# Attention backward on one core: O and wo transposed by DMA instead of TensorE, and half of K on TensorE

## The chip, the cores and the metric

One Trainium2 chip, one of its cores. The metric is the device time of one launch in microseconds, the median of several runs. The kernel is written by hand, with tiles, pools of buffers and an explicit order of emission; the time of before is the median of three runs on the chip.

## The reference

Two independent attention blocks A and B are computed forward and backward, and their outputs stand side by side. One block, for B = 8 batches, H = 32 heads, Sq = 96 queries, Sk = 512 cached keys, Dh = 128 and D = 640, all in bfloat16:

```
q   = (x @ wq) split into heads          # [8, 32, 96, 128]
s   = q @ k_cache^T * Dh**-0.5           # [8, 32, 96, 512]
p   = softmax(s)
o   = p @ v_cache                        # [8, 32, 96, 128]
out = concat of heads of o @ wo          # [8, 96, 640]
```

`reference()` returns the output (blocks side by side, [8, 96, 1280]) and, for a given `grad_out`, the gradients of x, k_cache, v_cache, wq and wo of both blocks. The gradients of the caches have the caches' size, 8 x 32 x 512 x 128 each, so the kernel reads some 161 MB from HBM and writes some 159 MB.

## The kernel before, in words

**Units of work.** A chunk is one head h and one batch b: 96 queries against 512 keys. The chunks run in the order of heads, and within a head of batches, first all of block A (32 heads), then all of block B. Time is divided into ticks; chunk n starts at tick n. The stages of one chunk are spread over several ticks, so that in each tick each engine works on several chunks at different stages (the table `OFF`): keys loaded 5 ticks ahead (`ldk`), values 3 ahead (`ldv`), S and softmax at tick 3 after the chunk's own (`c_s2a`, `c_s2b`, `c_s3a`, `c_s3b`), P transposed and dV at 4 (`c_s45`, `c_s4`), O at 5, dP and dS at 6 (`c_s6`), dK and dS transposed at 7 (`c_s7`, `c_s8`), dQ at 8 (`c_s8`). K and V come in pairs of batches, one DMA for two chunks.

**Order.** Every piece is added to `Emitter` with a tick and a slot within the tick, and the pieces are emitted in the order of (tick, slot). Each engine works its own instructions off in order, with two exceptions: S and softmax are raised in priority (`tc.high_priority`), and instructions in `pinned(...)` keep the program's place on their queue. DMAs of SP's queue are pinned: the loads of K and V (slot 0), the transposing DMAs (slot 1), the stores of dV and dK (slot 1.5), all of a tick before the next tick's.

**Transposes of K and V.** dP needs V transposed and S needs K transposed. V is always transposed by a DMA from SBUF to SBUF (`c_xt`, tile `VT`, one DMA for two chunks, at the tick of the first). For K, `k_on_pe(h, b)` decides: for the first pair of batches of each head, and for some whole heads at the start of a block, TensorE transposes it chunk by chunk (`c_s1`, four transposes of 128 x 128 into PSUM, copied by VectorE to `KT_pe`); the other pairs go by DMA (`KT`, issued three ticks ahead of the chunk's own).

**Work once per head.** Pieces with the slot `SL_HEAD` come after the chunk stages of a tick; their ticks (table `HK`) count from the head's first chunk. At -10 and -9 the head's parts of wq and wo are loaded from POOL's queue (`pA`, `pA2`; tile `wo_h`). At -3, `pB` transposes wo (five transposes into `woT_ps`, copied by ScalarE to `woT_h`) and wq (the same, by VectorE, to `wqT_h`). From -2 to 0, `pC` projects Q from wq and dO from `woT_h` (matmuls `q_ps`; dO's first 512 columns at tick -1). At 1 and 2, `pD` brings dO and Q to natural layout. After the head's chunks, `qA(h, 1)` at 17 and `qA(h, 0)` at 18 transpose dQ and O of the head to natural layout (six transposes each into `nat_ps`; O is copied by ScalarE to `Onat`, dQ by VectorE to `dQnat`). At 19 and 20, `qB` computes dwo from `Onat` (matmuls `dwo_ps`); at 18, 19 and 21, in odd heads, `qD` computes dwq for two heads. So in a steady state each tick belongs to a head's phase: tick t and tick t + 8 do the same work for consecutive heads, and tick -3 of the next head is tick 5, tick 18 of the last one is tick 2.

**Work once per group of heads.** Heads are taken in groups of at most five. After a group, `gU` multiplies the group's O with wo and dQ with wq (matmuls `o_ps`), adding into accumulators of out and dx; these pieces are spread over some 18 ticks, so that some heads have much of this work and others none.

**Buffers.** All matmul results go through eight banks of PSUM, used in rotation. `woT_h` and `Onat` have one buffer each; `KT` has three, `VT` four.

Of the kernel before, what the change touches and what calls it, by code (L numbers as in the profile page):

```python
# [11 lines left out]
BF16 = mybir.dt.bfloat16  # L12
# [28 lines left out]
SL_HEAD = 90  # L41
# [1 line left out]
SL_SETUP = 96  # L43

OFF = dict(ldk=-5, ldv=-3, kt=-3, vt=0, s2=3, s3=3, s4=4, s5=5, s6=6, s7=7, s8=8)
HK = dict(pA=-10, pA2=-9, pB=-3, pC0=[-2, 0], pC1=[-1, 0], pD1=1, pD0=2, qA0=18, qA1=17, qB=[19, 20], qD=[(18, 0, 2), (19, 2, 4), (21, 4, 5)])
EV = dict(pB0="act", pB1="dve", pC00="act", pC01="act", pC10="act", pC11="dve", pD0="dve", pD1="dve", qA0="act", qA1="dve", qB0="act", qB1="dve", qD="dve", gU="act")
GSPREAD0 = 9
PRIO_OFF = 2000
# [4 lines left out]
def build_block(tc, em, tick0, blk, x, kc, vc, wq, wo, g_all, out_all, dx, dk, dv, dwq, dwo, ident, ones, pools, HG=6, first=True, groups=None):  # L54
# [43 lines left out]
    def bank(shape, dt, name):  # L98
        return ps.tile(shape, dt, name=name, tag="bank")
# [11 lines left out]
    def pinned(ins):  # L111
        return tc.keep_in_program_order(ins)
# [42 lines left out]
    def evac(eng, dst, src, sc=None):  # L155
        if eng == "act":
            nc.scalar.activation(dst, src, ACT.Identity, scale=(1.0 if sc is None else sc))
        else:
            if sc is None:
                nc.vector.tensor_copy(dst, src)  # L160
            else:
                nc.vector.tensor_scalar(dst, src, float(sc), None, op0=ALU.mult)
# [33 lines left out]
    def pA2(h):  # L196
        def f():
            wo_h = hst.tile([128, D], BF16, name="wo_h", bufs=HG + 3)
            ld = nc.gpsimd.dma_start(wo_h[:], wo[h * 128:(h + 1) * 128, :])
            if not (first and h == 0):  # L200
                pinned(ld)
            HS[(blk, h)]["wo_h"] = wo_h
        return f

    def pB(h):
        def f():
            st = HS[(blk, h)]
            woT_ps = bank([128, DC * 128], BF16, "woT_ps")
            for c in range(DC):
                nc.tensor.transpose(woT_ps[:, c * 128:(c + 1) * 128], st["wo_h"][:, c * 128:(c + 1) * 128], ident[:])  # L210
            woT_h = hd.tile([128, DC * 128], BF16, name="woT_h", bufs=1)
            evac(EV["pB0"], woT_h[:], woT_ps[:])
            st["woT_h"] = woT_h
            wqT_ps = bank([128, DC * 128], BF16, "wqT_ps")
            for c in range(DC):
                nc.tensor.transpose(wqT_ps[:, c * 128:(c + 1) * 128], st["wq_h"][:, c, :], ident[:])
            wqT_h = hst.tile([128, D], BF16, name="wqT_h")
            evac(EV["pB1"], wqT_h[:], wqT_ps[:])
            st["wqT_h"] = wqT_h
            st["slot"] = (blk * H + h) % OD.shape[2]  # L220
            st["OT_h"] = OD[:, 0, st["slot"]]
            st["dQT_h"] = OD[:, 1, st["slot"]]
            st["QT_h"] = hd.tile([128, T], BF16, name="QT_h")
            st["dOT_h"] = hd.tile([128, T], BF16, name="dOT_h")
        return f
# [199 lines left out]
    def c_s7(h, b):  # L425
# [9 lines left out]
            nc.scalar.activation(SB[(blk, h, b // 2, "k")][:, b % 2], dK_ps[:], ACT.Identity, scale=1.0)  # L435
        return f

    def qA(h, which):
        def f():
            st = HS[(blk, h)]  # L440
            src = st["OT_h"] if which == 0 else st["dQT_h"]
            if which == 0:
                dst = hd.tile([128, TT, 128], BF16, name="Onat", bufs=1)
                st["Onat"] = dst
            else:
                if h % 2 == 0:
                    st["dQnat"] = hd.tile([128, TT, 2, 128], BF16, name="dQnat", bufs=1)
                else:
                    st["dQnat"] = HS[(blk, h - 1)]["dQnat"]
                dst = st["dQnat"][:, :, h % 2, :]  # L450
            for t0 in range(0, TT, 8):
                nt = min(8, TT - t0)
                n_ps = bank([128, 8 * 128], BF16, "nat_ps")
                for i in range(nt):
                    nc.tensor.transpose(n_ps[:, i * 128:(i + 1) * 128], src[:, (t0 + i) * 128:(t0 + i + 1) * 128], ident[:])  # L455
                evac(EV["qA%d" % which], dst[:, t0:t0 + nt, :], n_ps[:, 0:nt * 128].rearrange("p (t d) -> p t d", d=128))
        return f
# [88 lines left out]
    NTS = len(tsplits)  # L546

    def k_on_pe(h, b):
        return b // NB == 0 or h == 0 or (first and h == 1)

    SX = pools["SX"]
    for g in range(NG):
        h0 = GH0[g]
        for hh in range(groups[g]):
            h = h0 + hh
            c0t = tick0 + h * B
            if not (first and h == 0):
                em.add(c0t + HK["pA"], 54.6, pA(h))
                em.add(c0t + HK["pA2"], 54.6, pA2(h))
            em.add(c0t + HK["pB"], SL_HEAD, pB(h))  # L560
            fh = first and h == 0
            p0, p1, d1, d0, late = HK["pC0"], HK["pC1"], HK["pD1"], HK["pD0"], 0
            if fh:
                p1, d1, d0, late = [3, 3], 3, 4, 7
            elif h == 0:
                p0, p1, d1, d0, late = [-2, 2], [0, 3], 3, 4, 7
            for si in range(NTS):
                em.add(c0t + p0[min(si, 1)], SL_HEAD, pC(h, 0, si))
                em.add(c0t + p1[min(si, 1)], SL_HEAD + late, pC(h, 1, si))
            em.add(c0t + d1, SL_HEAD + (8 if late else 0), pD(h, 1))  # L570
            em.add(c0t + d0, SL_HEAD, pD(h, 0))
            for b in range(B):
                ct = c0t + b
                if b % NB == 0:
                    em.add(tick0 - 12 if first and h == 0 and b == 0 else ct + OFF["ldk"], SLOTS["LOAD"], c_ld(h, b, "K", 7))
                    em.add(ct + OFF["ldv"], SLOTS["LOAD"], c_ld(h, b, "V", 5))
                    if not k_on_pe(h, b):
                        em.add(ct + OFF["kt"], SLOTS["LOAD"] + 1, c_xt(h, b, "KT", 3))
                    em.add(ct + OFF["vt"], SLOTS["LOAD"] + 1, c_xt(h, b, "VT", 4))
                if k_on_pe(h, b):  # L580
                    em.add(ct + 2, SLOTS["S1"], c_s1(h, b))
                em.add(ct + OFF["s2"], SLOTS["S2A"], c_s2a(h, b))
                em.add(ct + OFF["s2"], SLOTS["S2B"], c_s2b(h, b))
                em.add(ct + OFF["s3"], SLOTS["S3A"], c_s3a(h, b))
                em.add(ct + OFF["s3"], SLOTS["S3B"], c_s3b(h, b))
                em.add(ct + OFF["s5"], SLOTS["S5B"], c_s5b(h, b))
                if b % 2 == 1:
                    em.add(ct + OFF["s4"] + 1, SLOTS["LOAD"] + 1.5, c_st(h, b, "v"))
                    em.add(ct + OFF["s7"] + 1, SLOTS["LOAD"] + 1.5, c_st(h, b, "k"))
                em.add(ct + OFF["s4"], SLOTS["S4"], c_s4(h, b))  # L590
                for i, o in enumerate(("s8", "s7", "s5", "s4")):
                    SX.setdefault(ct + OFF[o], [None] * 4)[i] = (blk, h, b)
                em.add(ct + OFF["s6"], SLOTS["S6"], c_s6(h, b))
                em.add(ct + OFF["s7"], SLOTS["S7"], c_s7(h, b))
            hk = HK if first or h < H - 1 else dict(HK, qA0=13, qB=[14, 15], qA1=16, qD=[(19, 0, 2), (19, 2, 4), (19, 4, 5)])
            em.add(c0t + hk["qA0"], SL_HEAD, qA(h, 0))
            for di in range(len(wsplits)):
                em.add(c0t + hk["qB"][di], SL_HEAD + 1, qB(h, di))
            em.add(c0t + hk["qA1"], SL_HEAD, qA(h, 1))
            for (k_, c_lo, c_hi) in hk["qD"]:  # L600
                if c_lo < DC and h % 2 == 1:
                    em.add(c0t + k_, SL_HEAD + 2, qD(h, c_lo, min(c_hi, DC)))
        cLg = tick0 + (h0 + groups[g] - 1) * B + B - 1
        gs0 = max(3, (GSPREAD0 * groups[g]) // HG)
        gs1 = max(3, (GSPREAD1 * groups[g]) // HG)
        if not first and g == NG - 2:
            gs0, gs1 = 9, 9
        if g == 0:
            em.add(cLg + OFF["s5"] - 2, SL_LOAD, setup_acc)
        subs = [(0, t, gi) for t in range(TT) for gi in range(len(gsplits))] + [(1, t, gi) for t in range(TT) for gi in range(len(gsplits))]  # L610
        n_out = TT * len(gsplits)
        for i, (which, t, gi) in enumerate(subs):
            if which == 0:
                tk = cLg + OFF["s5"] + 2 + (i * gs0) // n_out
            else:
                tk = cLg + OFF["s8"] + 2 + gs0 - 3 + ((i - n_out) * gs1) // n_out
            em.add(tk, SL_GRP, gU(g, which, t, gi))
# [124 lines left out]
```

## Time and profile before

| What | Value |
|---|---|
| Time, median of 3 runs | 1671.19 us (1670.91 to 1674.83) |
| Profiled execution, its own time | 1669.93 us |
| Its span, first to last instruction | 1668.1 us |
| Mean granted TensorE clock | 0.999 |
| TensorE matmuls (PE) | busy 1638.2 us, 98% of the span |
| TensorE weight loads (PEld) | busy 1318.2 us, 79% |
| VectorE (DVE) | busy 1303.1 us, 78% |
| ScalarE (ACT) | busy 1392.7 us, 83% |
| GpSimd (POOL) | busy 663.8 us, 40% |
| HBM | 161.09 MB read, 159.12 MB written |
| Transposing DMAs | 256 VT, 183 KT |
| Median from issue to landing | VT 5.1 us, KT 5.0 us, loads of K 4.3 to 4.4 us |

How to read it: busy time is the union of an engine's instructions, and a row of a group gives the busy time, the mean duration of one instruction in ns, and the idle time of the engine just before them with what ended it. Matmuls overlap, so the mean duration of one (219 ns for 128 columns) is longer than the distance to the next. DMA issues stand on the engine that issues them (SPq is SP's queue), with the time that the issuing took. A window's row has the length, the busy time and number of instructions of PE, PEld, DVE, ACT and POOL, the granted clock, the DMA engines' share and the rate in GB/s.

### The profile page before, as it was taken

How to read it: one execution, taken by the hardware profiler on the slowest of the kernel's cores; microseconds unless marked ns; L12 is line 12 of the kernel's file. 1: busy time of each engine (PE TensorE's matmuls, PEld its weight loads, DVE VectorE, ACT ScalarE, POOL GpSimd, SP SyncE). 2: the span in 40 equal slices, each digit the busy share in tenths (PEclk: the TensorE clock that was granted, in tenths of full speed). 3: DMA queues.
4: the chain of work that ended last, by engine and by line, in shares of the span. 5: the costliest groups of instructions: out<-in, count | busy, mean ns of one | idle time of the engine just before them, and what ended most of it. 6: DMA issues, size and time to landing. Idle time of an engine off the chain costs nothing.

```text
span 1668.1 us, 56047 instructions
## 1 busy us (share of the span) xinstructions
PE 1638.2 (98%) x21355; PEld 1318.2 (79%) x21536; DVE 1303.1 (78%) x2978; ACT 1392.7 (83%) x3518; POOL 663.8 (40%) x1235
## 2 busy tenths in 40 slices
PE   8999999999999999999999999999999999999998
PEld 7887787787788787887878778877877877877886
DVE  6886777778788788888888767878878778787787
ACT  7998897797798796978879898978977977977975
POOL 3444343343343343434344333433433433433432
PEclk9999999999999999999999999999999999999999
DMA  9999999999999999999999999999999999998994
GB/s 275 259 294 277 233 275 278 243 284 271 239 269 272 247 284 249 269 259 264 292 261 283 286 282 247 292 260 244 279 276 225 276 270 244 282 284 230 246 285 147
DMA packets 763151, 439.03 MB, mean 263 GB/s; under 512 B 483776, under 2 KB 753472, under 8 KB 762880
## 3 DMA queue, kind: packets, MB, share of 16 engines
q1 hardware_dynamic: 750256, 392.32, 98.9%
q0 software_dynamic: 12624, 43.10, 8.4%
q8 instruction: 169, 2.77, 0.7%
q14 instruction: 102, 0.84, 0.2%
HBM read 161.09 MB, written 159.12 MB: 192 GB/s over the span
## 4 chain that ended last, share of the span: by engine, by line
PE 81%; ACT 10%; issue 4%; DVE 3%; DMA 1%; POOL 0%; SPq 0%; ACTq 0%; DVEq 0%; POOLq 0%
PE q_ps L243 12%; PE o_ps L512 11%; PE dwq_ps L490 6%; PE dK_ps L432 6%; PE dV_ps L389 6%; PE dP_ps L417 5%; PE S_ps L298 5%; PE dst_ps L346 5%; PE dwo_ps L470 4%; PE x_ps L365 4%; PE x_ps L359 4%; PE x_ps L340 4%; PE n_ps L258 3%; PE nat_ps L455 2%; ACT E_sb L310 2%
## 5 line engine op out<-in xcount | busy, mean ns | idle before, releaser
L329 POOL TENSOR_SCALAR P_sb<-E_sb,rinv 96x512 bf16<-96x512 bf16 x512 | 352.2, 688 | 873.6 <-DVE rinv L320 842.6
L310 ACT ACTIVATE E_sb<-S_ps,negm 96x512 bf16<-96x512 f32 x512 | 353.5, 690 | 164.3 <-DVE negm L300 162.3
L421 DVE SCALAR_TENSOR_TENSOR dS_sb<-dP_ps,dl_ps,P_sb 96x512 bf16<-96x512 f32 x512 | 381.1, 744 | 47.3 <-PE dl_ps L419 42.9
L300 DVE TENSOR_REDUCE negm<-S_ps 96x1 f32<-96x512 f32 x512 | 347.7, 679 | 48.0 <-PE S_ps L298 45.7
L435 ACT ACTIVATE dK_sb<-dK_ps 128x512 bf16<-128x512 f32 x512 | 304.9, 595 | 73.6 <-PE dK_ps L432 72.6
L392 ACT ACTIVATE dV_sb<-dV_ps 128x512 bf16<-128x512 f32 x512 | 314.0, 613 | 0.0
L378 ACT ACTIVATE PT_sb<-x_ps 128x384 bf16<-128x384 bf16 x512 | 255.7, 499 | 0.0
L512 PEld LDWEIGHTS <-OD 128*128 128x128 bf16 x1536 | 135.7, 98 | 103.2 <-issue 1.3
L389 PE MATMUL dV_ps<-dOnat_h,P_sb 96*128 96x128 bf16 x2048 | 198.2, 219 | 1.3 <-DVE dOnat_h L160 0.6
L432 PE MATMUL dK_ps<-Qnat_h,dS_sb 96*128 96x128 bf16 x2048 | 198.1, 219 | 0.0
L417 PE MATMUL dP_ps<-VT,dOT_h 128*96 128x512 bf16 x512 | 195.2, 381 | 0.0
L407 POOL TENSOR_TENSOR prod<-OD,dOT_h 128x96 bf16<-128x96 bf16 x512 | 184.8, 361 | 8.9 <-ACT OD L375 8.6
L348 DVE COPY dST_sb<-dst_ps 128x384 bf16<-128x384 bf16 x512 | 177.3, 346 | 12.6 <-PE dst_ps L346 12.3
L320 DVE RECIPROCAL rinv<-rowsum 96x1 f32<-96x1 f32 x512 | 79.9, 156 | 130.3 <-ACT E_sb L310 125.5
L346 PE MATMUL dst_ps<-ident,dS_sb 96*128 96x96 bf16 x2048 | 172.0, 206 | 2.1 <-DVE dS_sb L421 0.2
L365 PE MATMUL x_ps<-ident,P_sb 96*128 96x96 bf16 x2048 | 171.9, 205 | 1.6 <-POOL P_sb L329 1.3
L375 ACT ACTIVATE OD<-x_ps 128x192 bf16<-128x192 f32 (+1 forms) x515 | 170.5, 331 | 3.4 <-PE x_ps L340 3.4
L359 PE MATMUL x_ps<-PT_sb,V_sb 128*128 128x96 bf16 x2048 | 172.4, 206 | 0.5 <-ACT PT_sb L378 0.5
L340 PE MATMUL x_ps<-dST_sb,K_sb 128*128 128x96 bf16 x2048 | 170.9, 206 | 0.0
L340 PEld LDWEIGHTS <-K_sb 128*128 128x128 bf16 x2048 | 132.7, 98 | 32.1
L298 PE MATMUL S_ps<-KT,QT_h 128*96 128x512 bf16 x366 | 138.7, 379 | 2.6 <-DMA KT<-K_sb 2.3
L512 PE MATMUL o_ps<-wo_h,OD 128*128 128x128 bf16 (+1 forms) x705 | 134.0, 292 | 3.3
(82 smaller groups left out, 3352.4 us busy)
## 6 DMA issues: line engine op xcount, KB each, us to landing
out_dram<-dV_sb SPq DMA_DIRECT2D x256, 256.0 KB, 4.1
out_dram<-dK_sb SPq DMA_DIRECT2D x256, 256.0 KB, 4.5
K_sb<-in_A_k_cache_dram SPq DMA_DIRECT2D x128, 256.0 KB, 4.4
V_sb<-in_A_v_cache_dram SPq DMA_DIRECT2D x128, 256.0 KB, 4.2
K_sb<-in_B_k_cache_dram SPq DMA_DIRECT2D x128, 256.0 KB, 4.3
V_sb<-in_B_v_cache_dram SPq DMA_DIRECT2D x128, 256.0 KB, 4.1
out_dram<-dwo_sb POOLq DMA_DIRECT2D x63, 160.0 KB, 3.9
out_dram<-dwq_sb POOLq DMA_DIRECT2D x31, 320.0 KB, 5.4
```

The source lines that it names most:

```text
L300: nc.vector.tensor_reduce(negm[:], S_ps[:], axis=AX.X, op=ALU.max, negate=True)
L310: nc.scalar.activation(E_sb[:], st["S_ps"][:], ACT.Exp, bias=st["negm"][:], scale=1.0, accum_out=rowsum[:])
L329: pinned(nc.gpsimd.tensor_scalar(P_sb[:], st["E_sb"][:], st["rinv"][:], 0.0, op0=ALU.mult, op1=ALU.add))
L340: nc.tensor.matmul(dQT_ps, st["K_sb"][:, c, :], st["dST_sb"][:, c * Sq:(c + 1) * Sq], start=(c == 0), stop=(c == KC - 1))
L378: nc.scalar.activation(PT_sb[:], PT_ps, ACT.Identity, scale=1.0)
L389: nc.tensor.matmul(dV_ps[:, c * 128:(c + 1) * 128], P_sb[:, c * 128:(c + 1) * 128], hs["dOnat_h"][:, b * 128:(b + 1) * 128], start=True, s ...
L392: nc.scalar.activation(SB[(blk, h, b // 2, "v")][:, b % 2], dV_ps[:], ACT.Identity, scale=1.0)
L417: nc.tensor.matmul(dP_ps[:], hs["dOT_h"][:, tok], st["VT"], start=True, stop=True)
L421: nc.vector.scalar_tensor_tensor(dS_sb[:], dP_ps[:], dl_ps[:, 0:1], st["P_sb"][:], op0=ALU.subtract, op1=ALU.mult)
L432: nc.tensor.matmul(dK_ps[:, c * 128:(c + 1) * 128], dS_sb[:, c * 128:(c + 1) * 128], hs["Qnat_h"][:, b * 128:(b + 1) * 128], start=True, s ...
L435: nc.scalar.activation(SB[(blk, h, b // 2, "k")][:, b % 2], dK_ps[:], ACT.Identity, scale=1.0)
L512: nc.tensor.matmul(o_ps[:], src[:, t * 128:(t + 1) * 128], rhs, start=(hh == 0), stop=(hh == groups[g] - 1))
```

## The change

Three things change.

- O is brought to natural layout by a transposing DMA on SP's queue (`qA_xt`, tick 14, slot 1.2), in place of six TensorE transposes and a copy by ScalarE in `qA(h, 0)` at tick 18. `qA` is left with dQ. In the last head of block B the DMA is at tick 13, and `qB` is at ticks 16 and 17 instead of 14 and 15.
- wo is transposed by a DMA on SP's queue (`pB_xt`, tick -4, slot 1.2), in place of five TensorE transposes and a copy by ScalarE in `pB` at tick -3; only the first two heads of block A keep the old way.
- `k_on_pe` takes the third pair of batches too, so that of each head batches 0, 1, 4 and 5 have K transposed by TensorE and copied by VectorE, and the DMA for that pair is not issued.

In numbers of instructions: 206 pairs of weight load and matmul fewer on TensorE, 126 activations fewer on ScalarE, 122 copies more on VectorE, 61 transposing DMAs of K fewer and 64 of O and 62 of wo more on SP. On SP the DMA of wo stands directly behind the one of V for batch 4, and the DMA of O directly behind that for batch 6.

```diff
-HK = dict(pA=-10, pA2=-9, pB=-3, pC0=[-2, 0], pC1=[-1, 0], pD1=1, pD0=2, qA0=18, qA1=17, qB=[19, 20], qD=[(18, 0, 2), (19, 2, 4), (21, 4, 5)])
+HK = dict(pBT=-4, pA=-10, pA2=-9, pB=-3, pC0=[-2, 0], pC1=[-1, 0], pD1=1, pD0=2, qT=14, qA1=17, qB=[19, 20], qD=[(18, 0, 2), (19, 2, 4), (21, 4, 5)])
...
+    def woT_on_pe(h):
+        return first and h < 2
+
+    def pB_xt(h):
+        def f():
+            woT_h = hd.tile([128, DC * 128], BF16, name="woT_h", bufs=1)
+            pinned(nc.sync.dma_start_transpose(woT_h[:].rearrange("p (c k) -> p c k", k=128), HS[(blk, h)]["wo_h"][:]))
+            HS[(blk, h)]["woT_h"] = woT_h
+        return f
+
     def pB(h):
         def f():
             st = HS[(blk, h)]
-            woT_ps = bank([128, DC * 128], BF16, "woT_ps")
-            for c in range(DC):
-                nc.tensor.transpose(woT_ps[:, c * 128:(c + 1) * 128], st["wo_h"][:, c * 128:(c + 1) * 128], ident[:])
-            woT_h = hd.tile([128, DC * 128], BF16, name="woT_h", bufs=1)
-            evac(EV["pB0"], woT_h[:], woT_ps[:])
-            st["woT_h"] = woT_h
+            if woT_on_pe(h):
+                woT_ps = bank([128, DC * 128], BF16, "woT_ps")
...
+    def qA_xt(h):
+        def f():
+            Onat = hd.tile([128, TT, 128], BF16, name="Onat", bufs=1)
+            pinned(nc.sync.dma_start_transpose(Onat[:], HS[(blk, h)]["OT_h"]))
+            HS[(blk, h)]["Onat"] = Onat
+        return f
...
     def k_on_pe(h, b):
-        return b // NB == 0 or h == 0 or (first and h == 1)
+        return b // NB in (0, 2) or h == 0 or (first and h == 1)
...
+            if not woT_on_pe(h):
+                em.add(c0t + HK["pBT"], SLOTS["LOAD"] + 1.2, pB_xt(h))
             em.add(c0t + HK["pB"], SL_HEAD, pB(h))
...
-            hk = HK if first or h < H - 1 else dict(HK, qA0=13, qB=[14, 15], qA1=16, qD=[(19, 0, 2), (19, 2, 4), (19, 4, 5)])
-            em.add(c0t + hk["qA0"], SL_HEAD, qA(h, 0))
+            hk = HK if first or h < H - 1 else dict(HK, qT=13, qB=[16, 17], qA1=16, qD=[(19, 0, 2), (19, 2, 4), (19, 4, 5)])
+            em.add(c0t + hk["qT"], SLOTS["LOAD"] + 1.2, qA_xt(h))
```

## The prediction

> **What bounds the kernel now.** I read the page first: parts 1 and 3 for who is busy, part 4 for the chain that ended last.
>
> ```profile
> span 1668.1 us, 56047 instructions
> ...
> PE 1638.2 (98%) x21355; PEld 1318.2 (79%) x21536; DVE 1303.1 (78%) x2978; ACT 1392.7 (83%) x3518; POOL 663.8 (40%) x1235
> ...
> q1 hardware_dynamic: 750256, 392.32, 98.9%
> ...
> PE 81%; ACT 10%; issue 4%; DVE 3%; DMA 1%; POOL 0%; SPq 0%; ACTq 0%; DVEq 0%; POOLq 0%
> ```
>
> TensorE holds the chain and DMA is only 1% of it, yet the hardware queue's packets fill 98.9% of 16 engines. Both have to be read finer. A busy PE can still be waiting, so I took the distance from each matmul's start to the next from the trace: 42 ns for 96 columns, 55 for 128, 136 for 320, 216 for 512. All matmuls at these distances make about 1614 us of the 1668; waits that show as longer distances add to only some 43 us, 10 of them at the start. So TensorE is the bound, and its columns can be counted at full price. The second view is the groups that the change touches, by shape (mean ns of one after the bar):
>
> ```profile
> L157 ACT ACTIVATE Onat<-nat_ps 128x768 bf16<-128x768 bf16 x64 | 52.4, 819 | 0.0
> L157 ACT ACTIVATE woT_h<-woT_ps 128x640 bf16<-128x640 bf16 x64 | 45.6, 713 | 0.0
> L287 DVE COPY KT_pe<-kT_ps 128x512 bf16<-128x512 bf16 x146 | 59.7, 409 | 2.2 <-PE kT_ps L285 2.1
> L285 PE MATMUL kT_ps<-ident,K_sb 128*128 128x128 bf16 x584 | 56.6, 219 | 0.0
> L455 PE MATMUL nat_ps<-ident,OD 128*128 128x128 bf16 x768 | 63.4, 218 | 1.1
> L210 PE MATMUL woT_ps<-ident,wo_h 128*128 128x128 bf16 x320 | 28.1, 218 | 0.0
> ```
>
> The third is the timeline of SP's queue against TensorE. A head is eight ticks. In heads without gU a head takes 21.4 to 23.0 us (starts of S_ps eight chunks apart), in heads with much gU up to 30.4. The DMA work of a head is the same in all of them, so in the light heads SP falls behind and in the heavy ones it catches up: the time from KT's landing to the S_ps that reads it swings between about 16 and 4 us, once per group of five heads. At the end of a light stretch it looks like this:
>
> ```profile
> 516.88 2.69 SPq L275 DMA_TRANSPOSE VT<-V_sb  x1
> 519.67 0.53 SPq L398 DMA_DIRECT2D out_dram<-dV_sb  x1
> ...
> 519.69 1.24 PE L243 MATMUL q_ps<-gT,woT_h 128*128 128x512 bf16 x5
> ```
>
> This VT is the one of tick 4, behind which the change puts the transpose of wo; the q_ps that follows is the first reader of woT, in tick 7. SP is free of VT at 519.57 and the reader starts at 519.69.
>
> **TensorE, taken away and added.** Removed: 64 x 6 transposes of O and 62 x 5 of wo, 694. Added: 61 heads x 2 chunks x 4 of K, 488. 206 fewer x 55 ns = -11.4 us, all on the engine that sets the end.
>
> **ScalarE and VectorE.** ScalarE loses 64 x 819 and 62 x 713 ns, 97 us; it mostly waits for VectorE's negm or for TensorE, so I count only the bank waits ahead of the first nat_ps in tick 2 (4 us in all, from the distances), of which half stay with the next user of that bank: -2, between -4 and 0. VectorE gains 122 copies x 409 ns = 50 us in ticks 6 and 7, where it is idle 0.8 and 1.2 us of some 3.2; TensorE's extra 0.22 us there covers part. New waits for banks in these ticks: 0, between -5 (the dst_ps that waits for dS in tick 6 is filled by K's transposes) and +6 (0.05 us in 61 heads, twice). In tick 5 five transposes go, and the dS that dst_ps of tick 6 needs comes no earlier: +1.
>
> **Where TensorE's saving is not worth its price.** Tick 2 loses the six transposes of O, 0.33 us, but there VectorE is the limit:
>
> ```profile
> 353.21:356.87 3.66, 3.66 (x68) 3.46 (x67) 3.66 (x10) 3.51 (x9) 1.39 (x4) 1.00 1.08 247
> ...
> 357.57 0.16 PE L419 MATMUL dl_ps<-ones,prod 128*96 128x1 bf16 x1
> 357.78 0.30 PE L470 MATMUL dwo_ps<-g_nat,Onat 128*128 128x320 bf16 x1
> ```
>
> Third figure of the window: VectorE, busy without a gap from negm of tick 2 to the end of negm of tick 3. dwo_ps then starts 0.21 us after dl_ps instead of 0.03: its bank is S_ps's, which E_sb frees after that negm. Heads with this pattern (neither gU nor qD in tick 2) are 18 of 60; there the 0.33 us only lengthens the wait: +6 us, between 0 (VectorE finds other gaps) and +12 (twice as many heads).
>
> **The DMA path.** KT loses 61 transposes of 1024 rows; O adds 64 of 768 and wo 62 of 640: per head 384 rows of 256 B more. A whole transpose took 1.48 us of the engines' time on average (651 us with transposes in flight over 439) and 0.9 in an undisturbed stretch: 0.34 to 0.56 us per head, against the 1.5 to 2.5 us by which a light head already falls behind. I take 0.5. The Trainium skill, Advanced Engine Details and Errata, X-Bar Transpose (TRN2), gives transposes the speed of ordinary DMAs, 350 to 400 GB/s; the mean here is 177. By that rule the 96 KB would cost about 0.27 us, an estimate, and the waits below would come out some 3 us smaller.
>
> Behind this lies a new wait. Before, woT came from TensorE itself in tick 5 and could not be late. Now tick 7's q_ps waits for a DMA, and all of TensorE stands in order behind it. For each of 62 heads I took the time from the end of VT's issue in tick 4 to the first reader of woT: median 6.6 us, in the lowest tenth under 1.6, least -3.2. What woT needs after that point is its own issue, 0.77 us by rows of 1.23 for a 1024-row transpose, and the 3.28 us (median) from end of issue to landing that a VT takes: some 4.0 us. In stretches in which less is left, the largest shortfalls are 2.2, 2.5, 0.7, 3.9, 7.2, 2.2 and 4.4 us, 23 together; one number for a stretch, because a wait gives DMA the same time back. The missing KT (tick 1) helps and the earlier O and wo hurt, net some 0.8 us at the end of a stretch: +7 over the nine or so stretches that then cross. Sum +30, between 0 (DMA gains on SP once a KT is gone) and +60 (2 us in each of about 30 light heads). That gain on heavy heads does not come back: there TensorE is the bound and DMA idles. Of O, needed in tick 19 after tick 14, at least 6.2 us is left after VT's issue where it needs some 4.2, so it hides; with that cover gone it would cost like wo. Behind the two new transposes on SP stand a store of dV and then the loads of K and V of the next tick; K is now read by TensorE seven ticks after its load, and landed at least 4.6 us ahead of that, so half a microsecond more of queue hides. wo_h, loaded from POOL's queue, landed 2.4 us or more before tick 4 begins in every head (median 4.4), so its new reader on SP does not wait for it; if it did, V and K would wait behind it. In the last head qB moves from ticks 14 and 15 to 16 and 17: the same work, in a tail where TensorE has little else, 0 with 1 us either way. The one long wait for KT, at 939 to 942 us, falls into the 7.2 us stretch and is counted there: -4 with its aftermath:
>
> ```profile
> 941.69 0.59 PE L298 MATMUL S_ps<-KT,QT_h 128*96 128x512 bf16 x1 [2.31 <-DMA KT<-K_sb]
> ...
> 942.00:945.00 3.00, 3.00 (x29) 2.65 (x28) 1.54 (x4) 1.49 (x4) 0.66 (x1) 0.50 0.95 307
> ```
>
> After 2.3 us of waiting the granted clock was 0.50 for 3.4 us, which costs 1.7 us more. Seven or eight stretches with a wait of 2 us or more would lose up to 14 us; I take five, +8, between 0 and 14. The Trainium skill, TensorE: Matmul & The Clock Gate, Why this matters for your kernels, warns of idle gaps above about 3 us; this gap was shorter and was punished. By the rule alone most of the 8 us would drop out.
>
> **Sum.** -11.4 + 6 + 1 - 2 + 0 + 30 - 4 + 8 = +27.6 us. The profiled execution took 1669.93 us, 1.8 beyond its span and 1.3 below the median of 1671.19. 1669.9 + 27.6 = 1697.5; on the scale of the median about 1698.
>
> **Rivals.**
> - *woT is in time, TensorE's count decides* (faster). It needs SP to reach tick 4 no more than some 5 us late: for it, a KT just before is gone; against it, lags of 7 to 10 us at 133, 261, 517 and 937 us. Without the DMA terms the sum is -6.4, 1665; with VectorE not binding either, -12.4, 1659. It decides if woT lands within the 4.0 us in every stretch. Chance 0.25.
> - *The two cancel.* Waits of 5 to 12 us in all against -6.4: 1668 to 1675. Chance 0.13.
> - *DMA becomes the bound.* A stop in each light head (60 us) and most clock drops: 1669.9 - 6.4 + 60 - 4 + 14 = 1733. For it the 98.9%; against it the gaps in heavy heads. Chance 0.07.
> - Forecast: 1676 to 1724, chance 0.55.
>
> **How the numbers follow.** About 0.3% (5 us) is what a measurement of this kernel can tell from no change: below 1666 faster, 0.25; to 1676 same, 0.13; above slower, 0.62 with the third rival. The range runs from 1660, leaving out the best ends of the first rival (0.08), to 1724, leaving out the third (0.07).
>
> **What would show it.** Right: waits of q_ps for a DMA woT<-wo_h of 1 to 7 us at the end of light stretches, several windows with half the clock, and none such in heavy heads; kT_ps x1072, nat_ps x384, woT_ps x10; ScalarE some 97 us less busy; dwo_ps still waiting in the 18 heads. Wrong: woT landing microseconds ahead of q_ps everywhere, with matmul distances as before; then the first rival holds. If KT or V are what TensorE waits for instead, the price of the added transposes was too low.

## The result and the profile after

The changed kernel takes 1715.99 us (median of 4 runs, 1715.36 to 1720.87) against 1672.86 us (4 runs, 1670.91 to 1674.83) for the kernel before, side by side on one chip: a ratio of 1.0267, 95% interval 1.0245 to 1.0290. It is slower, by more than the 1.7% of the forecast. The profiled execution took 1716.21 us, 1.8 beyond its span, so it compares with the 1669.93 us of before: 46.3 us more.

The page of the changed kernel, the span, part 1, part 3 and part 4:

```profile
span 1714.4 us, 56103 instructions
...
PE 1659.4 (97%) x21330; PEld 1311.2 (76%) x21330; DVE 1346.8 (79%) x3100; ACT 1330.5 (78%) x3392; POOL 668.2 (39%) x1235
...
q1 hardware_dynamic: 778704, 399.08, 99.6%
...
PE 81%; DMA 6%; ACT 5%; DVE 4%; issue 3%; POOL 0%; SPq 0%; ACTq 0%; DVEq 0%; POOLq 0%
```

PE's busy time went up although TensorE has fewer matmuls: a matmul at half clock counts as busy for longer, and the trace of before lacks some 210 records of matmuls with 512 columns (distances of twice 216 ns with nothing waited for), this one under 30. The share that speaks is DMA's in the chain, from 1% to 6%. The groups by shape show that the edit did what it says: O's transposes are gone from `nat_ps`, wo's are ten, K's have almost doubled, and ScalarE is 62 us less busy by part 1 (not the 97 us of the removed copies; part 1 counts overlapping instructions once, and nothing hangs on the difference):

```profile
L296 PE MATMUL kT_ps<-ident,K_sb 128*128 128x128 bf16 x1072 | 103.7, 219 | 0.0
L298 DVE COPY KT_pe<-kT_ps 128x512 bf16<-128x512 bf16 x268 | 109.7, 410 | 9.2 <-PE kT_ps L296 9.0
L469 PE MATMUL nat_ps<-ident,OD 128*128 128x128 bf16 x384 | 31.7, 218 | 0.0
L221 PE MATMUL woT_ps<-ident,wo_h 128*128 128x128 bf16 x10 | 0.9, 219 | 0.0
L254 PE MATMUL q_ps<-gT,woT_h 128*128 128x512 bf16 x320 | 91.2, 403 | 36.5 <-DMA woT_h<-wo_h 35.8 <-ACT gT L157 0.6
```

The last row is the new cost. In the waits of PE (total, times, longest) it stands first, and the one wait for KT of before has shrunk to 0.5:

```profile
PE q_ps L254 <- DMA woT_h<-wo_h: 35.8, 16, 6.7
PE S_ps L309 <- DMA KT<-K_sb: 0.5, 1, 0.5
```

The longest of the sixteen, in the timelines of SP's queue and of PE (start, length, then the instruction):

```profile
1371.81 1.23 SPq L286 DMA_TRANSPOSE KT<-K_sb  x1
1373.13 1.22 SPq L409 DMA_DIRECT2D out_dram<-dK_sb  x1
1374.40 2.58 SPq L286 DMA_TRANSPOSE VT<-V_sb  x1
1377.08 1.32 SPq L211 DMA_TRANSPOSE woT_h<-wo_h  x1
1378.48 1.04 SPq L409 DMA_DIRECT2D out_dram<-dV_sb  x1
```

```profile
1375.37 0.16 PE L430 MATMUL dl_ps<-ones,prod 128*96 128x1 bf16 x1
1382.20 2.31 PE L254 MATMUL q_ps<-gT,woT_h 128*128 128x512 bf16 x5 [6.67 <-DMA woT_h<-wo_h]
1384.31 0.63 PE L526 MATMUL o_ps<-wo_h,OD 128*128 128x512 bf16 x1
```

TensorE was ready for woT at 1375.5. SP was then still issuing VT, took up wo only at 1377.08, and the data landed 5.1 us later. The windows of that stretch (length, busy time of PE, PEld, DVE, ACT, POOL, granted clock, DMA share, GB/s) show what a stop of TensorE does:

```profile
1376.00:1379.00 3.00, 0.00 (x0) 0.00 (x0) 0.50 (x1) 1.22 (x4) 1.57 (x3) 0.74 0.82 164
1379.00:1382.00 3.00, 0.00 (x0) 0.00 (x0) 0.00 (x0) 0.00 (x0) 0.00 (x0) 0.50 1.19 333
1382.00:1385.00 3.00, 2.80 (x7) 1.09 (x8) 0.00 (x0) 0.44 (x1) 0.00 (x0) 0.50 1.13 360
1385.00:1388.00 3.00, 3.00 (x21) 1.73 (x20) 1.57 (x4) 0.93 (x3) 0.01 (x1) 0.55 1.12 336
```

From 1379 to 1382 nothing computes and the DMA engines are full. The granted clock fell to 0.50 at 1377.5, during the wait, and stayed there until 1387.7, so that TensorE's first 5.5 us after the wait run at half clock.

**Where the 46 us are.** As in the prediction, the distance from each matmul's start to the next was taken from the trace, less the distance that its columns need (twice that where the clock was 0.50; the columns of missing records are counted with the others):

| us | before | after | difference |
|---|---|---|---|
| columns at full clock | 1612.6 | 1600.7 | -11.9 |
| waits for woT and KT over 0.3 us | 2.5 | 38.7 | +36.2 |
| lost to half clock | 1.5 | 13.5 | +12.0 |
| all other waits | 46.3 | 56.2 | +9.9 |

### The profile page after: what moved, and what is told of

Same layout as the page of the kernel before. It is cut to its first block, busy times and chain, and to the rows that moved or that the text cites. A ratio compares the mean times of both kernels' runs of the same rounds, so it can differ in the third digit from the quotient of the medians.

```text
span 1714.4 us, 56103 instructions
## 1 busy us (share of the span) xinstructions
PE 1659.4 (97%) x21330; PEld 1311.2 (76%) x21330; DVE 1346.8 (79%) x3100; ACT 1330.5 (78%) x3392; POOL 668.2 (39%) x1235
## 4 chain that ended last, share of the span: by engine, by line
PE 81%; DMA 6%; ACT 5%; DVE 4%; issue 3%; POOL 0%; SPq 0%; ACTq 0%; DVEq 0%; POOLq 0%
PE q_ps L254 12%; PE o_ps L526 11%; PE dwq_ps L504 6%; PE dK_ps L443 6%; PE S_ps L309 6%; PE dV_ps L400 5%; PE dP_ps L428 5%; PE dwo_ps L484 5%; PE dst_ps L357 5%; DMA woT_h<-wo_h 5%; PE x_ps L370 4%; PE x_ps L376 4%; PE x_ps L351 4%; PE n_ps L269 3%; PE kT_ps L296 3%
## 5 line engine op out<-in xcount | busy, mean ns | idle before, releaser
L321 ACT ACTIVATE E_sb<-S_ps,negm 96x512 bf16<-96x512 f32 x512 | 348.9, 681 | 222.3 <-DVE negm L311 213.6
L446 ACT ACTIVATE dK_sb<-dK_ps 128x512 bf16<-128x512 f32 x512 | 300.1, 586 | 73.7 <-PE dK_ps L443 69.6
L403 ACT ACTIVATE dV_sb<-dV_ps 128x512 bf16<-128x512 f32 x512 | 308.9, 603 | 0.0
L389 ACT ACTIVATE PT_sb<-x_ps 128x384 bf16<-128x384 bf16 x512 | 250.5, 489 | 0.0
L254 PE MATMUL q_ps<-gT,woT_h 128*128 128x512 bf16 (+1 forms) x640 | 142.3, 338 | 37.1 <-DMA woT_h<-wo_h 35.8
L386 ACT ACTIVATE OD<-x_ps 128x192 bf16<-128x192 f32 (+1 forms) x515 | 165.4, 321 | 3.8 <-PE x_ps L351 3.8
L526 PE MATMUL o_ps<-wo_h,OD 128*128 128x128 bf16 (+1 forms) x768 | 144.9, 305 | 0.0
```

Of the source, the lines that this page charges most:

```text
L254: nc.tensor.matmul(q_ps[:], lhs(c), rhsT[:, c, t0:t0 + w], start=(c == 0), stop=(c == DC - 1))
L321: nc.scalar.activation(E_sb[:], st["S_ps"][:], ACT.Exp, bias=st["negm"][:], scale=1.0, accum_out=rowsum[:])
L403: nc.scalar.activation(SB[(blk, h, b // 2, "v")][:, b % 2], dV_ps[:], ACT.Identity, scale=1.0)
L526: nc.tensor.matmul(o_ps[:], src[:, t * 128:(t + 1) * 128], rhs, start=(hh == 0), stop=(hh == groups[g] - 1))
```

## The experiments

The theory behind the forecast: in heads without gU SP and DMA fall behind, and woT, issued last in tick 4, is needed before it lands. Rivals: the rows that DMA has to transpose cost what they cost wherever they stand; or VectorE and ScalarE do. Each ratio is against the kernel before on the same chip. Kernels 1 to 4, 5 to 8, 9 to 11 and 12 ran on four chips, on which the kernel before had medians of 1670.1 to 1671.8 us; a difference in microseconds between kernels of different groups goes across chips. The twelve kernels below are numbered as they ran.

**1. wo early.** Undo the lateness: wo is transposed three ticks earlier, and wo and wq are loaded three ticks earlier for it.

```diff
-HK = dict(pBT=-4, pA=-10, pA2=-9, ...
+HK = dict(pBT=-7, pA=-13, pA2=-12, ...   # wo_h: HG + 4 buffers, woT_h: 2
```

> The changed kernel, with wo's transpose issued three ticks earlier (tick -7, where the change dropped a KT) instead of behind VT in tick -4; wo and wq are loaded three ticks earlier too, with one buffer more for wo_h and for woT_h. TensorE's, VectorE's and ScalarE's instructions and the number of DMA rows stay the same. Lateness theory (the extra time is q_ps waiting for a transpose issued too late in light heads, 38 us in the matmul distances, plus some 16 us of half clock after those waits): 1716 - 38 - 16 = 1662 us, no wait of q_ps for woT over 1 us, at most two half-clock windows. DMA-load rival (the 384 rows more per head are what TensorE pays for, wherever they stand): at least 1700 us, the waits moving to VT, KT or K. Rival of VectorE and ScalarE (negm in tick 2 and the 122 more evictions in ticks 6 and 7 are the cost): about 1700, waits on negm, dS and dl grown.

1682.07 us (1675.46 to 1686.18), ratio 1.0073 [1.0047, 1.0099]. The waits for woT are gone, 34 us are back, and a quarter of the loss is left. KT now is late in the profiled run, which was the second longest of the five (1686.00):

```profile
PE S_ps L309 <- DMA KT<-K_sb: 10.5, 10, 2.8
```

So lateness is the larger part, and neither theory is whole: with one transpose out of the way, a smaller wait stands at the next. Four windows of half clock cost 6 us more; one of them follows no KT but a wait of 3.7 us for a load (`ld_tmp`) at the change of blocks.

**2. wo back on TensorE.**

```diff
     def woT_on_pe(h):
-        return first and h < 2
+        return True
```

> The changed kernel with wo transposed by TensorE and evicted by ScalarE again; O stays on DMA and K stays half on TensorE. Lateness theory: 1716 - 38 - 16 + 310 x 0.055 = 1679 us; no long DMA wait. DMA-load rival: about the same or lower, 1675 to 1680, since this kernel has 256 rows a head fewer than the one before. VectorE rival: 1690 or more, since the evictions of K stay.

1679.98 us, ratio 1.0060 [1.0038, 1.0081], no DMA wait over 0.3 us behind the start and no half clock. The count (TensorE's columns +5.3 us over before) and the other waits (+7.5, by the same distances), less the KT wait and the half clock of before, give it. The time fits both forecasts, 1679 us by lateness and 1675 to 1680 by the load of DMA; of the rivals only VectorE's (1690 or more) falls here.

**3. Half of K on TensorE, nothing else.** The kernel before with `b // NB in (0, 2)` in `k_on_pe`.

> The kernel before with half of K instead of a quarter transposed on TensorE, and nothing else. 488 transposes x 55 ns = +26.8 us, the one KT wait with its half clock gone (-4): 1671 + 23 = 1694 us. If VectorE's 122 added copies cost (VectorE rival): over 1700. If the 1024 rows a head fewer relieve TensorE of more than that one wait (DMA-load rival): below 1688.

1692.03 us, ratio 1.0131 [1.0113, 1.0149]. The count alone: columns +26.5, other waits -0.3. VectorE's 122 copies cost nothing, and its rival falls for ticks 6 and 7.

**4. O alone by DMA.** The changed kernel with `woT_on_pe` True and `k_on_pe` as before.

> The kernel before with O alone transposed by DMA (wo on TensorE, K a quarter on TensorE). 384 transposes x 55 ns = -21.1 us, VectorE-bound tick 2 +6, dS +1, banks -2: 1655 us, if the 768 rows a head more hide. Lateness theory: they push KT and VT later by 0.7 us a light head at the one place where KT already had no slack, 2 to 6 waits of 1 to 3 us with some half clock: 1660 to 1670. DMA-load rival: the lag grows in every light head: 1680 or more, with waits on KT and VT.

1671.73 us in ten runs, ratio 1.0022 [0.9988, 1.0056]; but these runs spread from 1662.12 to 1686.21, where 14 runs of the kernel before on that chip lie between 1667.88 and 1674.11. The median lies between the forecasts (1660 to 1670, and 1680 or more). The profiled run, the second shortest of the ten, took 1664.86:

```profile
PE S_ps L309 <- DMA KT<-K_sb: 6.3, 6, 2.4
```

TensorE's columns fell by 21.9 us; in that run DMA waits and other waits (+10.4 us) took most of it back. In the median run, which has no profile, all of it was gone.

**5. wo ahead of VT instead of behind it**, in tick -4 still.

```diff
-em.add(c0t + HK["pBT"], SLOTS["LOAD"] + 1.2, pB_xt(h))
+em.add(c0t + HK["pBT"], SLOTS["LOAD"] + 0.9, pB_xt(h))
```

> The changed kernel with wo's transpose issued just ahead of VT in tick -4 instead of just behind it; nothing else. Lateness theory: woT gains the VT's issue (1.2 to 3.2 us) in each of its 16 waits (35.8 us, mean 2.2), so most of them go and with them half of the half-clock windows: 1716 - 25 - 8 = 1683 us; VT becomes later by the issue of wo (0.8 us) where it had 2.8 us left, so no wait for VT. DMA-load rival (a late light head costs the same whatever is issued first): above 1705, the waits for woT only a little shorter or moved to VT or KT.

1696.45 us (1685.96 to 1705.31), ratio 1.0147 [1.0115, 1.0179]. The median gained 20 us, some 60% of what the theory gave it. The profiled run was the longest of the four (1705.31) and still waits for woT 13 times, with 28.7 us; neither VT nor KT is waited for. The direction holds: one place earlier in SP's order pays.

**6. and 7. K's loads and KT one tick earlier**, on kernels 1 and 4.

```diff
-OFF = dict(ldk=-5, ldv=-3, kt=-3, ...
+OFF = dict(ldk=-6, ldv=-3, kt=-4, ...   # K: 8 buffers
```

> The kernel with early wo (first experiment) whose K loads and KT transposes are issued one tick earlier still (-6 and -4 for -5 and -3), with 8 buffers of K for 7, 2 of KT for 3 and 1 of woT. Same instructions, same DMA rows. Headroom theory (a light stretch runs up a debt of DMA time that heavy heads pay back; a transpose issued a tick earlier is ahead of that debt): the ten KT waits of 10.5 us in all, longest 2.8, and the four half-clock windows go: 1682 - 10.5 - 6.5 = 1665 us. Load rival (DMA is full on the average, headroom is used up and waits return): above 1678, with as many waits, on KT or VT.

> O alone by DMA (fourth experiment), with K loads and KT transposes one tick earlier and one buffer of K more. Headroom theory: its six KT waits (6.3 us) and most of its spread of 1662 to 1686 us go, 1655 to 1660 us, faster than the kernel before. Load rival: no gain, 1665 to 1680, spread as wide.

1695.42 us, ratio 1.0159 [1.0135, 1.0183], and 1750.22 us, ratio 1.0461 [1.0423, 1.0498]: 13 and 78 us slower than kernels 1 and 4. Neither theory says this: the headroom theory has the wrong sign, and the load rival, whose "above 1678" holds for kernel 6, looked for the waits at KT and VT. In both kernels the longest waits are for O, in kernel 6 16.1 us and in kernel 7:

```profile
PE dwo_ps L484 <- DMA Onat<-OD: 55.4, 25, 3.7
```

SP's timeline shows that the edit did two things at once (in kernel 6 four: KT has also two buffers for three there, and woT one for two). The earlier tick is an even one, and there KT stands directly behind VT:

```profile
507.82 2.43 SPq L286 DMA_TRANSPOSE VT<-V_sb  x1
510.35 3.04 SPq L286 DMA_TRANSPOSE KT<-K_sb  x1
513.44 1.28 SPq L452 DMA_TRANSPOSE Onat<-OD  x1
```

Over all 183 KT the issue takes 2.40 us on average in kernel 7 and 1.43 in kernel 4, where loads and not a transpose stand ahead. With headroom and neighbours changed together, the headroom theory stays untested; what it gave is a new suspicion, the order of transposes on SP. Onat, directly behind a VT, has 1.93 us in kernel 1 and 2.13 in kernel 4; woT, 1.39 behind VT in the changed kernel and 1.35 behind direct DMAs in kernel 1, shows no such effect. Nor do VT behind woT (1.52 in kernel 5, 1.74 for the other VT there) and Onat as the third transpose in a row, behind KT (1.58 in kernel 7).

**8. DMA only in heavy heads.** K a quarter on TensorE; wo (early) and O by DMA where the transpose falls into a head full of gU, by TensorE elsewhere. The expectation says 26 heads each; the trace has 24 transposes of wo and 25 of O by DMA.

> K a quarter on TensorE as before; wo (early) and O by DMA only where the transpose falls into a head full of gU (26 heads each), by TensorE and ScalarE in the others. 270 transposes fewer on TensorE, -14.9 us. Lateness theory with room in heavy heads: no wait for woT or Onat, KT waits as in the kernel before or one or two more: 1671 - 15 + 1 = 1657 us. Load rival (DMA has no room in heavy heads either): KT waits as in the O-alone kernel, 1665 or more.

1674.63 us in twelve runs, ratio 1.0014 [0.9994, 1.0034], no gain, as the load rival said. The profiled run, the longest of the twelve (1681.33), has 14 KT waits of 15.0 us, mostly at the ends of light stretches again (112, 513, 522, 908, 957 us and so on). One reading is that the room in heavy heads is not free but the lead on which the next light stretch lives. It rests on where the waits stand, not on a run made for it, and it has a rival: each O stands directly behind a VT here and each wo directly behind a KT, an order of which the next two kernels remove O's part. The heavy heads weren't tried with another order.

**9. and 10. O away from VT.** O's transpose in tick 13 instead of 14 (`qT=13`), on kernels 1 and 4; no two transposes are neighbours any more.

> The kernel with early wo (first experiment) with O's transpose moved from tick 14, where it stands directly behind a VT on SP, to tick 13, where only direct DMAs stand ahead of it. Same instructions, same rows; no two transposes are neighbours any more. Issue theory (SP's time is what runs out in a light head, and a transpose directly behind a transpose holds SP longer: Onat 1.93 us behind VT, woT 1.35 behind direct DMAs): SP gets back some 0.6 us a head, about 2 us at the end of a light stretch, and most of the ten KT waits (10.5 us) and four half-clock windows go: 1682 - 12 = 1670 us. Rows theory (the DMA engines' work is what runs out): no change, 1682.

> O alone by DMA (fourth experiment), with O's transpose moved from tick 14 to tick 13, away from VT. Issue theory: Onat's issue falls from 2.13 us to about 1.4, the six KT waits (6.3 us) and the spread of 1662 to 1686 us mostly go: median 1660 us, faster than the kernel before. Rows theory: no change, median 1672 with the same spread.

1673.32 us, ratio 1.0008 [0.9989, 1.0026], and 1661.98 us (1656.49 to 1667.89), ratio 0.9946 [0.9924, 0.9967]: 9 and 10 us better than kernels 1 and 4, and kernel 10 beats both the kernel before and the changed one. Onat's issue fell to 1.45 and 1.34 us, as the issue theory asked. That SP got this time back is seen in kernel 9 alone: its transposes took 845 us to issue in all, for 877 in kernel 1. In kernel 10 it was 856 for 858 in kernel 4: VT's issue rose from 1.80 to 1.97 us on average. So the times came as the theory said, and its reason is not shown. The waits of PE in kernel 10:

```profile
PE S_ps L309 <- DMA KT<-K_sb: 4.8, 9, 1.0
```

Nine for six in kernel 4, but none over 1.0 us where one had 2.4, and no half clock within the run, where kernel 4 had one window of it. Place and neighbour were moved together here too; that the tick alone, without the neighbour, would have done it isn't excluded.

**11. VT in halves.** The kernel before with one VT a head issued as two transposes of 512 rows, a store between them: one instruction more a head on SP, no row more.

> The kernel before with one of the four VT transposes of a head issued as two of 512 rows, a store of dV between them; same rows, one transpose instruction more a head on SP, nothing else. Issue theory: a transpose costs SP at least 1.2 us whatever its rows, so a head costs SP 0.7 to 1.2 us more, 2 to 4 us at the end of a light stretch: KT waits at several of them, 1675 to 1690 us. Rows theory: 1671 us, the one KT wait as before.

1672.07 us, ratio 1.0012 [0.9996, 1.0028]. SP's transposes took 66 us more to issue (823 for 757), and by the interval the kernel lost between nothing and 5 us. The time is that of the rows theory; but the profiled run (1678.02, the second longest of the ten) doesn't have "the one KT wait as before":

```profile
PE S_ps L307 <- DMA KT<-K_sb: 6.5, 3, 3.5
```

So one microsecond of issue more a head, at this place, is nearly free in the median run; that it never makes KT late isn't shown.

**12. Everything by DMA**, K still a quarter on TensorE.

> O and wo both by DMA with K still a quarter on TensorE: wo early (tick -7, behind the store of dK), O in tick 13, so that no two transposes are neighbours. 694 transposes fewer on TensorE than before, 1408 rows a head more on DMA (the O-alone kernel has 768 more). Room theory (DMA still has room in heavy heads, and lag is only a matter of order): 1662 - 310 x 0.055 = 1645 us, KT waits under 10 us. Rows theory (each added row brings the debt of a light head nearer to TensorE): 20 to 40 us of waits for KT, VT or K and 10 us or more of half clock, 1675 to 1700 us.

1737.19 us, ratio 1.0394 [1.0371, 1.0417]. To kernel 10 it adds the 62 transposes of wo by DMA. TensorE has 17 us less to do than there, and the kernel takes 75 us more:

```profile
PE S_ps L309 <- DMA KT<-K_sb: 55.8, 27, 4.9
```

Another 28 us go to half clock. The room theory is wrong, and the loss is larger than the rows theory expected. But the expectation says that no two transposes are neighbours, and SP's timeline shows otherwise: in 61 heads the VT of the next tick stands directly behind wo.

```profile
515.20 1.70 SPq L211 DMA_TRANSPOSE woT_h<-wo_h  x1
516.99 1.33 SPq L286 DMA_TRANSPOSE VT<-V_sb  x1
```

These VT don't take longer to issue (1.60 us on average, the others 1.93). Still, rows, the number of transposes on SP (940 us of issue for 856) and the order changed together, and which of them cost the 75 us is open. That a light head's debt grows with each row, and that each row is paid for once the lead is gone, would explain it and is not shown.

Taken together: TensorE's waits for KT, VT, woT and Onat above 0.3 us, from the distances of one profiled run each, by the rows that a head adds to the kernel before (kernel 8, which adds them in some heads only, has 18.4 us).

| rows a head | us of waits (kernel) |
|---|---|
| -1024, -256 | none (3, 2) |
| 0 | 2.5 (the kernel before), 7.3 (11) |
| +384 | 38.7 (the changed kernel), 30.5 (5), 19.9 (6), 14.1 (1), 8.5 (9) |
| +768 | 68 (7), 9.8 (4), 8.1 (10) |
| +1408 | 67 (12) |

With the same rows the place on SP decides over a factor of four to eight. With the best places tried, 384 and 768 rows cost about the same 8 us, and kernel 11 has 7.3 with none; only the step to 1408 is steep, and there order and issue changed too.

## Why the prediction was right in its direction and too small

The mechanism is the predicted one. q_ps waits for woT at the ends of light stretches, the clock falls at half of these waits, TensorE's saving doesn't cover them. Term by term, on the scale of the profiled executions:

| Term | predicted | measured |
|---|---|---|
| TensorE's columns | -11.4 | -11.9 |
| woT, less the KT wait that it takes over | +30 - 2.3 | +36.2 |
| half clock, less that of before | +8 - 1.7 | +12.0 |
| VectorE in tick 2, dS, banks, ticks 6 and 7 | +6 + 1 - 2 + 0 | +9.9 |
| sum | +27.6 | +46.2 |

**The wait for woT** was sized too small in one step: "some 4.0 us" from the end of VT's issue to woT's landing, applied to every stretch. Over the 46 heads that don't wait it is 3.96 us; in the 16 that do it is 5.01. The extra microsecond lies behind woT's issue: from its end to the landing 3.57 us there, 2.45 elsewhere, while the issue itself takes 1.33 and 1.41. VT's issue, just ahead, takes 2.36 us there and 1.60 elsewhere, so SP and DMA are late together. A median over all heads was used for the moments in which the queue is full. One microsecond on each of sixteen waits is some 16 of the 38.0 us that the waits came to.

Part of the nearness is luck. For heads that don't wait 4.0 is right because two errors cancel: the issue was taken in proportion to the rows (0.77 us for 1.41; it has a floor, see below) and the landing from VT (3.28 for 2.45). And +30 stood for nine waits of 3.3 us each, one a stretch; sixteen came, of 2.4 us on average. The prediction's 1697.5 us, by the way, are 1698.8 on the scale of the median, not 1698, and its rivals' times mix the two scales, which lie 1.3 us apart.

**The load of DMA** was put at 0.34 to 0.56 us a head, taken as 0.5. The time with transposes in flight (their packets starting no more than 20 ns apart) rose from 651 to 691 us, 0.62 a head, above that range. The mean rate of transposes stayed at 176 GB/s (177 before). The Trainium skill, Advanced Engine Details and Errata, X-Bar Transpose (TRN2), expects 350 to 400 GB/s; beside this kernel's other traffic the transposes don't get that, and an estimate by that rule would have made the sum smaller still. That "DMA idles" in heavy heads doesn't fit the trace of before either: the DMA engines' share was 1.17 and 0.91 in two heads with gU (276.5 to 306.9 and to 332.3 us), 1.17 and 1.16 in the two without it that follow.

**Half clock.** Five windows were taken, eight came, one of them 10.24 us long. Which waits are followed by half clock is no matter of length alone: 1.79 and 1.95 us in kernel 1 were followed by half clock, 2.05 us (at 407) and 2.93 us (at 915) in the changed kernel weren't. All half-clock periods inside the runs last 3.41 us or two or three times that. The Trainium skill, TensorE: Matmul & The Clock Gate, What's actually happening, speaks of a free-running window of 3413 ns. The lengths agree with that. Its bound of idle gaps over some 3 us (section Why this matters for your kernels) doesn't agree with the waits of 1.79 and 1.95 us.

**VectorE in tick 2** was wrong in place, and the group of four terms to which it belongs, +5 in all, was half of the +9.9 measured. The wait of dwo_ps, which was to grow by 6 us in 18 heads, shrank instead, from 5.9 us in 28 places to 2.7 in 11. What grew are short waits in ticks 3 to 5: of dl_ps for its input (0.4 to 3.9 us), of S_ps behind the n_ps of Q (3.1 more), of the transposes of P for POOL (2.8 to 5.9). That these come with O's move is shown by one profiled run each: kernel 10, where only O moved, has them too (other waits +9.7 us in all), and in kernel 3, where only K did, other waits fall by 0.3. A fourth group comes with wo: q_ps waits 19 times for some 0.17 us behind dl_ps until E_sb frees its bank, 3.5 us for 0.5 before. Kernels 1 and 5 have it too, kernels 2 and 10, where wo stays on TensorE, don't. It is the kind of wait that the prediction priced for dwo_ps, at another matmul, and about what lies between the 9.9 here and the 7.5 of kernel 2, which has the same O and K. Why the gaps opened at these places and not at dwo_ps was not tested.

**O's DMA hides** was true for O, with no wait of dwo_ps for it in the changed kernel, and not for its neighbours: moving it to another tick, away from VT, was worth 9 and 10 us (kernels 9 and 10). The prediction asked whether O would be in time. Of what stands behind O's 1.89 us on SP it looked at the loads of K alone and found room; in kernels 1 and 4 it was KT that came late.

**The rivals.** "woT is in time" fell with the first page. "The two cancel" fits kernel 9 (8.5 us of waits, 1673 us). Nearest to "DMA becomes the bound" comes kernel 12, with 67 us of waits, though several light heads wait for nothing there.

## What to carry to other kernels

- Moving work from the engine that sets the end to one that is nearly full is priced where that one is latest, not on the average: take latencies from the stretches in which its queue is behind (here 5.0 us for 4.0), and don't count the room in other stretches as free before a run has shown it (in experiment 8 it bought nothing).
- A value that the engine made itself just before can't be held up by a DMA queue; once it comes by DMA, ask at which place of the issuing queue it stands. The same transposes at other places were worth 34 us (wo) and 10 us (O), and the one part of the change that paid (O alone, away from VT, 0.5%) was hidden in the sum of three.

## What the runs showed of the hardware

- Issuing a transposing DMA on SP has a floor that hardly depends on its size: the least was 1.19 us for 512 rows, 1.20 for 640, 1.21 for 768 and 1.23 for 1024. Directly behind VT, KT took 2.40 us on average (kernel 7) and Onat 1.8 to 2.1, behind direct DMAs 1.43 (KT, kernel 4) and 1.34 to 1.45 (Onat). It is no rule for every transpose behind another: woT behind VT took 1.39 us, VT behind woT 1.52 and 1.60 (kernels 5 and 12), Onat behind KT 1.58 (kernel 7).
- A kernel in which some KT come late scatters: O alone by DMA spread over 24 us in ten runs, the same kernel with O one tick earlier over 11 us in six on another chip; the kernel before, with one late KT in its profile, spread over 6 and 10 us beside them.
